# A block kernel of attention and gated feed-forward: its down-projection by seven half-width products, with both LayerNorms of the second branch fed from the chip

## The chip, the cores and the metric

The kernel runs on one core of a Trainium2 chip. The metric is device time in microseconds (us). The five engines have short names in the profile: PE (TensorE; PEld is its weight load), DVE (VectorE), ACT (ScalarE), POOL (GpSimd) and SP (SyncE, which here issues the DMAs).

## The reference

An input of 2048 tokens by 512 columns goes through attention and a gated feed-forward network, each behind a LayerNorm with learned modulation from a condition vector `c`. Keys and values are the last 512 of a cache.

```python
mod = (silu(c) @ w_mod).reshape(1, 6, 1, -1)          # sa, ca, ga, sb, cb, gb
h = layernorm(x) * (1 + ca) + sa
q = h @ wq                                            # 32 heads of 128; 8 key/value heads
p = softmax(q @ k.T * 128 ** -0.5)                    # 512 keys, no mask
x = x + ga * ((p @ v) @ wo)                           # wo: 4096 x 512
h = layernorm(x) * (1 + cb) + sb
x = x + gb * ((gelu(h @ w_gate) * (h @ w_up)) @ w_down)   # feature width 1792
```

## The kernel before

**Numbers.** Every fp32 operand of a matmul is split into a high and a low fp16 half, and each product is three matmuls of 128x128 weights by 512 columns (`mm3`, lines 85 to 88): low by high, high by low, high by high.

**Attention.** The work goes in T = 512 slots of one score tile (128 queries by 512 keys) each, in two halves of 1024 tokens. Slot order is written out by hand for all engines: `at(slot, ...)` puts steps into a slot, `sched(...)` also plans a load into one of five `raw` buffers or two `rw` buffers ahead of it, and three pieces of other PE work are popped in a slot: query projections (seven products in place of eight, on 2x2 blocks), probability by value, and the output projection `y_tasks`. Its sum is added to the accumulator tiles `acc` (128 tokens by 512, eight at a time) on DVE (line 876). When a tile has its last head, `attn_final` stores it as `y1` and later reloads the slot. SP issues all DMAs in program order, so one that waits for its data holds those behind it.

**Work for later stages inside attention.** From slot 286 on, every 27 slots, a pair `n` of feature blocks is prepared: `prep_set` for the gate and the up weights (POOL combinations and splits), `prep_wd` for two row blocks of `w_down`, all stored in DRAM (`kept`). LayerNorm tiles of the first half (`ln_tile` with gen 2) are planned in the same slots: each reloads `y1`, goes through statistics, normalisation on DVE, four PE transposes, modulation on ACT (`affine`), a store to `hs`, and splits. `combos` then makes the sums and differences of the token blocks that the seven products need. Columns of the modulation are made by `mod_load` at slots given in line 1081.

**Feed-forward.** There are 14 pairs: NP = 7 pairs of feature blocks, in each of two passes of 1024 tokens. A pair has two gate/up halves `q` (gate, then up), each of seven products of six matmuls (`f_items`, order 1, 2, 6, 7, 5, 4, 3). GELU runs between ACT and DVE, and the results are split into `at` tiles, keyed 11 and 21 (first token block), 12 and 22 (second). The down-projection of a pair is eight `y_tasks`, one for each 128-token tile, of six 512-column matmuls; `y_next` places one after four of the seven products of a half (line 1523). In the first pass the LayerNorm tiles and combinations of the second 1024 tokens (gen 3) are made too: reload of `y1`, statistics, and so on, with the combinations from gate product 7 on. In this stage the order on all engines but SP is set by the compiler's list scheduling; SP's stays as written. `f_final` stores a finished tile and hands its slot to the next reload. Eight PSUM banks are tagged `acc` (5), `s` (2) and `qa` (1).

Of the kernel before, what the change touches and what calls it, by code (L numbers as in the profile page):

```python
# [63 lines left out]
def block_kernel(ctx: ExitStack, tc: tile.TileContext, x, kT, v, wq, wo, wg, wu, wd, cT, wc, wm, out):  # L64
# [377 lines left out]
    xn = {}  # L442

    def ln_tile(gen, i, src):
# [20 lines left out]
        def affine(dts):  # L465
            if 0 in dts:
                st["f"] = tmp("hf")
# [5 lines left out]
            if KT - 1 in dts:  # L473
                dma(spilled(gen, qb)[:, :, i * P:(i + 1) * P], f.rearrange("p (k q) -> p k q", k=KT))
# [13 lines left out]
        return load, [stat, norm, turn, lambda: affine((0, 1)), lambda: affine((2, 3))] + more  # L488
# [309 lines left out]
    def banks(st, tags):  # L798
        def bk(k):
            def get():  # L800
                if k not in st:
                    st[k] = bank(*tags[k])
                return st[k]
            return get
# [77 lines left out]
    def attn_final(ti):  # L882
# [3 lines left out]
        at(now[0] + 3, lambda: load_acc(nxt, rows_of(x, nxt) if ti < 2 * QT else y1[nxt]))  # L886
# [194 lines left out]
    for j, ts_ in ((3, (257, 261, 265, 269)), (4, (259, 263, 267, 271)), (5, (274, 278, 282, 286))):  # L1081
# [5 lines left out]
    at(("w", 272), lambda: mx.update(m=mod_max(3)))  # L1087
    at(274, lambda: mod_scale(3, "mf", 1.0, mx["m"]))
# [24 lines left out]
    plan_gen(2, [T // 2 + 32 + 27 * (i // 2) + 11 * (i % 2) for i in range(8)], 478, 10, lambda i: y1[i])  # L1113
# [55 lines left out]
    B, A, G = {}, {}, {}  # L1169
# [9 lines left out]
    def f_items(q, hold=None):  # L1179
# [27 lines left out]
        def result(key, src):  # L1207
# [3 lines left out]
            else:  # L1211
                g = G.pop((n, key))
                nc.vector.scalar_tensor_tensor(g, g, 0.5 * GU, src, op0=ALU.mult, op1=ALU.mult)
                t = pair("ot", "at", NOT)
                nc.scalar.activation(t[:, 0, :], g, AF.Copy)
                nc.vector.tensor_tensor(t[:, 1, :], g, t[:, 0, :], op=ALU.subtract)
                A[n, key] = t
# [29 lines left out]
        tags = {"a": ("s", "fa", 2) if q else ("qa", "fa", 1), "b": ("acc", "fb", NACC), "c": ("acc", "fc", NACC)}  # L1247
        return with_posts(("f", q), 2 + q // (2 * NP), banks(st, tags), after)

# [51 lines left out]
    def prep_wd(n, b):  # L1301
        m, st = {}, {}
        outs = [staged() for _ in range(2)]
# [17 lines left out]
        def make(k):  # L1321
            nc.gpsimd.tensor_tensor(st[k], st[k], m["g"], op=ALU.mult)
            halves(outs[k][0]["t"], st[k])

        sched(b, (lambda: load(0), [lambda: stat(0), nop]), b + 7)
        sched(b + 1, (lambda: load(1), [lambda: stat(1), spread, nop]), b + 4, b + 9)
# [9 lines left out]
    for k in range(2):  # L1336
        at(T - 1 + 2 * k, lambda k=k: WO.update({("f", 0, k): fetch(("wd", 0, k), get_wo())}))
# [138 lines left out]
    load_later = []  # L1476
# [13 lines left out]
    for n in range(1, 2 * NP):  # L1490
        for k in range(2):
            f_at(2 * n + 1, 2 * k, lambda n=n, k=k: WO.update({("f", n, k): fetch(("wd", n % NP, k), get_wo())}))
# [74 lines left out]
```

## Time and profile before

| | |
|---|---|
| median of 3 runs | 1769.49 us (1769.39 to 1770.97) |
| profiled execution | 1767.57 us, span 1765.8 us, clock 1.000 |
| last accumulator tile of attention stored (`y1`) | issued at 1370.9 us |
| DVE busy, span | 1442.3 us (82%) |
| ACT busy, span | 1210.3 us (69%) |
| DMA | 329.71 MB, mean 187 GB/s |

The page gives for each engine the busy time within the span, then the span in 40 slices, the DMA queues, the chain of work that ended last, and groups of like instructions with their busy time, the mean of one and the idle time before them. A matmul's duration in the profile is its latency, and matmuls overlap, so their pace is read from start to start. Other views give the same quantities for a stretch of the span, a list in order of time, and who waited for whom.

### The profile page before, as it was taken

To read this page: it belongs to the slowest core of one execution; us is meant where nothing else is said; L and a number is where in the kernel's file an instruction comes from. 1 tells how busy PE (TensorE), PEld (TensorE's weight loads), DVE (VectorE), ACT (ScalarE), POOL (GpSimd) and SP (SyncE) were. 2 spreads that over 40 slices of the span, in tenths; PEclk is the share of its full clock that TensorE was granted. 3 is DMA by queue.
4 is the path that set the end of the run, shared out by engine and by line. 5 is a ranking of instruction groups with operands and counts; after the bars stand their busy time and mean duration, and the time that the engine had idled before them with its cause. 6 is when DMAs were issued, how large, how long until landed. Compare 5 with 4: busy or idle time off the path is not lost.

```text
span 1765.8 us, 25953 instructions
## 1 busy us (share of the span) xinstructions
PE 1730.5 (98%) x8112; PEld 796.0 (45%) x8114; DVE 1442.3 (82%) x2517; ACT 1210.3 (69%) x2814; POOL 875.9 (50%) x1095
## 2 busy tenths in 40 slices
PE   7899999999999999999999999999999999999999
PEld 5444444444444444444444444444444444444443
DVE  7888888888888888988888888888885867766676
ACT  6887787878778777677878777777773455434342
POOL 4879878776788872235475465565520033000000
PEclk9999999999999999999999999999999999999999
DMA  7999998999999989998999999999985543252222
GB/s 230 211 196 212 214 217 200 223 203 219 217 217 229 205 186 196 205 225 200 236 205 219 234 214 200 223 207 208 198 171 141 182 146 111 69 188 75 86 75 75
DMA packets 663273, 329.71 MB, mean 187 GB/s; under 512 B 553184, under 2 KB 575968, under 8 KB 663136
## 3 DMA queue, kind: packets, MB, share of 16 engines
q1 hardware_dynamic: 662848, 327.53, 80.2%
q8 instruction: 64, 1.05, 0.2%
q14 instruction: 73, 0.60, 0.1%
q10 hardware_dynamic: 288, 0.52, 0.1%
HBM read 133.83 MB, written 59.90 MB: 110 GB/s over the span
## 4 chain that ended last, share of the span: by engine, by line
PE 76%; DVE 11%; ACT 5%; POOL 3%; issue 3%; DMA 2%; SPq 0%; POOLq 0%; ACTq 0%; DVEq 0%
PE py L86 7%; PE py L87 7%; PE py L88 7%; PE ps L86 5%; PE ps L88 5%; PE ps L87 5%; PE po L86 4%; PE po L87 4%; PE po L88 4%; DVE p L925 3%; PE fa L86 3%; PE fa L88 2%; PE fa L87 2%; DVE nm L899 2%; PE qa L86 2%
## 5 line engine op out<-in xcount | busy, mean ns | idle before, releaser
L908 ACT ACTIVATE ee<-ps,nm 128x512 f32<-128x512 f32 x512 | 351.2, 686 | 254.1 <-DVE nm L899 244.4
L925 DVE SCALAR_TENSOR_TENSOR p<-ee,rr,p 128x512 f16<-128x512 f32 x512 | 463.4, 905 | 0.2
L899 DVE TENSOR_REDUCE nm<-ps 128x1 f32<-128x512 f32 x512 | 348.8, 681 | 73.5 <-PE ps L88 72.0
L920 ACT ACTIVATE p<-ee,rr 128x512 f16<-128x512 f32 x512 | 365.2, 714 | 1.7 <-DMA pt<-p 1.4
L86 PE MATMUL ps<-k,qt 128*128 128x512 f16 x512 | 194.1, 379 | 16.5 <-DVE qt L668 13.1
L86 PE MATMUL py<-wo,ot 128*128 128x512 f16 x512 | 194.1, 379 | 1.6 <-DVE ot L668 1.6
L86 PE MATMUL po<-pt,v 128*128 128x512 f16 x512 | 194.1, 379 | 0.1
L87 PE MATMUL po<-pt,v 128*128 128x512 f16 x512 | 194.0, 379 | 0.0
L88 PE MATMUL po<-pt,v 128*128 128x512 f16 x512 | 194.0, 379 | 0.0
L87 PE MATMUL py<-wo,ot 128*128 128x512 f16 x512 | 194.0, 379 | 0.0
L88 PE MATMUL py<-wo,ot 128*128 128x512 f16 x512 | 194.0, 379 | 0.0
L88 PE MATMUL ps<-k,qt 128*128 128x512 f16 x512 | 194.0, 379 | 0.0
L87 PE MATMUL ps<-k,qt 128*128 128x512 f16 x512 | 193.9, 379 | 0.0
L916 DVE RECIPROCAL rr<-rr 128x2 f32<-128x2 f32 x256 | 41.5, 162 | 102.7 <-ACT rr L913 101.3
L386 POOL TENSOR_TENSOR rs<-rs,nhalf 128x1 f32<-128x1 f32 x32 | 19.6, 611 | 194.1 <-DVE rs L380 191.5
L86 PEld LDWEIGHTS <-w 128*128 128x128 f16 x728 | 71.2, 98 | 88.4 <-DMA w<-kept 2.9
L87 PEld LDWEIGHTS <-w 128*128 128x128 f16 x728 | 71.2, 98 | 87.3 <-issue 2.7
L88 PEld LDWEIGHTS <-w 128*128 128x128 f16 x728 | 71.2, 98 | 86.0 <-issue 0.2
L876 DVE SCALAR_TENSOR_TENSOR acc<-py,dysc,acc 128x512 f32<-128x512 f32 x112 | 81.6, 746 | 28.8 <-PE py L88 28.0
L876 DVE SCALAR_TENSOR_TENSOR acc<-py,ysc,acc 128x512 f32<-128x512 f32 x128 | 94.6, 739 | 10.9 <-PE py L88 10.9
L908 ACT ACTIVATION_READ_ACCUMULATOR ee<-ps,nm 128x1 f32 x512 | 100.7, 197 | 0.0
L668 DVE SCALAR_TENSOR_TENSOR ot<-po,ot 128x512 f16<-128x512 f32 x128 | 86.9, 679 | 0.0
(263 smaller groups left out, 3817.1 us busy)
## 6 DMA issues: line engine op xcount, KB each, us to landing
w<-kept SPq DMA_DIRECT2D x123, 256.0 KB, 3.2
wo<-kept SPq DMA_DIRECT2D x60, 256.0 KB, 3.6
raw<-in_wo SPq DMA_DIRECT2D x56, 256.0 KB, 3.2
kept<-stage SPq DMA_DIRECT2D x56, 256.0 KB, 3.4
kept<-w SPq DMA_DIRECT2D x39, 256.0 KB, 3.4
rw<-in_wq SPq DMA_DIRECT2D x38, 256.0 KB, 3.3
hs<-hf SPq DMA_DIRECT2D x32, 256.0 KB, 2.7
pt<-p SPq DMA_TRANSPOSE x512, 3.5
```

The source lines that it names most:

```text
L86: nc.tensor.matmul(ps, llo, rhi, start=first, stop=False, skip_group_check=chain)
L87: nc.tensor.matmul(ps, lhi, rlo, start=False, stop=False, skip_group_check=chain)
L88: nc.tensor.matmul(ps, lhi, rhi, start=False, stop=last, skip_group_check=chain)
L386: nc.gpsimd.tensor_tensor(st["rs"], st["rs"], nhalf, op=ALU.pow)
L668: return lambda: nc.vector.scalar_tensor_tensor(t[:, 1, :], src, scale, t[:, 0, :], op0=ALU.mult, op1=ALU.subtract)
L876: nc.vector.scalar_tensor_tensor(acc[ti], st["p"], by, acc[ti], op0=ALU.mult, op1=ALU.add)
L899: nc.vector.tensor_reduce(nm, E[t]["ps"], axis=AX.X, op=ALU.max, negate=True)
L908: nc.scalar.activation(e, E[t]["ps"], AF.Exp, bias=E[t]["nm"], scale=1.0, accum_out=sm[:, t % 2:t % 2 + 1])
L916: return lambda: nc.vector.reciprocal(r, r)
L920: nc.scalar.activation(p16[:, 0, :], E[t]["e"], AF.Copy, scale=E[t]["r"])
L925: nc.vector.scalar_tensor_tensor(p16[:, 1, :], E[t]["e"], E[t]["r"], p16[:, 0, :], op0=ALU.mult, op1=ALU.subtract)
```

## The change

The down-projection of the first six pairs of each pass (`seven(n)`) is done on 2x2 blocks as well: two token blocks, two feature blocks, and two halves of 256 output columns, with seven products instead of eight. `y_sums` forms the four combinations of the results on POOL, `split` makes their fp16 halves on ACT and POOL, and `y_seven` is the list of 14 pieces of six matmuls of 256 columns for a pair, one placed after every product of the next halves from the fifth step on. Three of seven sums are copied from PSUM by ACT and added by POOL in two parts; four are added by DVE, one piece later (`defer`). PSUM banks of the long chains go round `qa`, `s`, `s`. `prep_wd` makes the four combinations of `w_down` and stores four tiles instead of two; the slots of the preparation move.

LayerNorm tiles of gen 2 take the accumulator tile itself, in place, 1 to 13 slots after `attn_final`, with normalisation on ACT; the reload of that slot moves from 3 to 12 slots behind. For gen 3 the statistics are taken at the end of attention (`ln_last`) and kept in `kmax` and `kinv`; normalisation is on ACT. Modulation columns 3 and 4 move from slots 257 to 271 to slots 211 to 229. In the feed-forward stage, the gen 3 stores, the first pass's outputs and its accumulator reloads are put off by 3, 2 and 5 product steps (`put_off`, `tick`), and the gen 3 combinations are spread by 2.5 steps instead of 2.

```diff
...
...
+    def tick():
+        for x in waits_:
+            x[0] -= 1
+        for x in [x for x in waits_ if x[0] <= 0]:
+            waits_.remove(x)
+            x[1]()
+    def ln_last(i):
+        st = {}
+        ln_stat(acc[2 * QT + i], st)
+        ln_power(st)
+        rs, nm = col("kmax", i), col("kinv", i)
+        pool_ts(rs, st["rs"], 1.0)
+        pool_ts(nm, st["mv"][:, 0:1], st["rs"], -1.0)
...
-            st["x"] = raw("xs")
-            dma(st["x"], src())
+            if gen == 2:
+                st["x"] = src()
+            else:
+                st["x"] = raw("xs")
+                dma(st["x"], src())
         def stat():
             ln_stat(st["x"], st)
             ln_power(st)
+            if gen == 2:
+                st["nm"] = small.tile([P, 1], F32, name="nmean")
+                pool_ts(st["nm"], st["mv"][:, 0:1], st["rs"], -1.0)
         def norm():
+            if gen == 3:
+                rs, nm = col("kmax", qb * QT + i), col("kinv", qb * QT + i)
+                return nc.scalar.activation(st["x"], st["x"], AF.Identity, bias=nm, scale=rs)
+            if gen == 2:
+                return nc.scalar.activation(st["x"], st["x"], AF.Identity, bias=st["nm"], scale=st["rs"])
             nc.vector.tensor_scalar(st["x"], st["x"], st["mv"][:, 0:1], st["rs"], op0=ALU.subtract, op1=ALU.mult)
...
-                st["f"] = tmp("hf")
+                st["f"] = raw("hf") if gen == 2 else tmp("hf")
...
+                def spill():
+                    dma(spilled(gen, qb)[:, :, i * P:(i + 1) * P], f.rearrange("p (k q) -> p k q", k=KT))
+                if gen == 3:
+                    put_off(3, spill)
+                else:
+                    spill()
...
+            own, steps = ln_tile(2, ti, lambda: acc[ti])
+            own()
+            for d, fn in zip((1, 6, 8, 9, 10, 12, 13), steps):
+                at(("w", now[0] + d), fn)
+            at(now[0] + 12, lambda: load_acc(nxt, rows_of(x, nxt)))
+        else:
+            ln_last(ti - 2 * QT)
+            at(now[0] + 3, lambda: load_acc(nxt, y1[nxt]))
...
+    for j, ts_ in ((3, (211, 215, 223, 227)), (4, (213, 217, 225, 229)), (5, (274, 278, 282, 286))):
         for dt in range(KT):
...
+    at(("w", 232), lambda: mx.update(m=mod_max(3)))
+    at(234, lambda: mod_scale(3, "mf", 1.0, mx["m"]))
...
-    plan_gen(2, [T // 2 + 32 + 27 * (i // 2) + 11 * (i % 2) for i in range(8)], 478, 10, lambda i: y1[i])
+    for p in range(2):
+        sched_combos(2, p, 482 + 10 * p)
...
+    def seven(n):
+        return n % NP < NP - 1
...
+        g11, g21, g12, g22 = (R.pop((n, k)) for k in ("11", "21", "12", "22"))
+        nc.gpsimd.tensor_tensor(g22, g12, g22, op=ALU.add)
+        nc.gpsimd.tensor_tensor(g12, g11, g12, op=ALU.subtract)
+        nc.gpsimd.tensor_tensor(g11, g22, g11, op=ALU.subtract)
+        nc.gpsimd.tensor_tensor(g21, g21, g11, op=ALU.subtract)
+        box = {}
+        def split(k, src):
+            if "t" not in box:
+                box["t"] = pool.tile([P, 4, 2, QB], F16, tag="pt", name="as", bufs=NPT)
+            t = box["t"][:, k]
+            nc.scalar.activation(t[:, 0, :], src, AF.Copy)
+            nc.gpsimd.tensor_tensor(t[:, 1, :], src, t[:, 0, :], op=ALU.subtract)
+            A[n, f"s{k + 1}"] = t
+        for i, (k, src) in enumerate(((0, g22), (1, g11), (3, g21), (2, g12))):
+            at(("f", 2 * n + 2, 1 + i), lambda k=k, src=src: split(k, src))
...
-                nc.vector.scalar_tensor_tensor(g, g, 0.5 * GU, src, op0=ALU.mult, op1=ALU.mult)
-                t = pair("ot", "at", NOT)
-                nc.scalar.activation(t[:, 0, :], g, AF.Copy)
-                nc.vector.tensor_tensor(t[:, 1, :], g, t[:, 0, :], op=ALU.subtract)
-                A[n, key] = t
+                dst = src if seven(n) and key != "21" else get_qt32() if seven(n) else g
+                nc.vector.scalar_tensor_tensor(dst, g, 0.5 * GU, src, op0=ALU.mult, op1=ALU.mult)
+                R[n, key] = dst
+                if not seven(n) or key != "12":
+                    t = pair("ot", "at", NOT)
+                    nc.scalar.activation(t[:, 0, :], dst, AF.Copy)
+                    nc.vector.tensor_tensor(t[:, 1, :], dst, t[:, 0, :], op=ALU.subtract)
+                    A[n, key] = t
+                if seven(n) and key == "12":
+                    y_sums(n)
...
-        tags = {"a": ("s", "fa", 2) if q else ("qa", "fa", 1), "b": ("acc", "fb", NACC), "c": ("acc", "fc", NACC)}
+        tags = {"a": chain_tag, "b": ("acc", "fb", NACC), "c": ("acc", "fc", NACC)}
...
+    def chain_tag():
+        chains[0] += 1
+        return (("qa", "fa", 1), ("s", "fa", 2), ("s", "fa", 2))[(chains[0] - 1) % 3]
...
+            if not seven(n):
+                halves(outs[k][0]["t"], st[k])
+            elif k == 0:
+                halves(outs[0][0]["t"][:, :, l], st[0][:, l])
+            else:
+                halves(outs[1][0]["t"], st[1])
+                combine()
...
+        def combine():
+            tt(st[0][:, l], st[0][:, r], st[0][:, l])
+            tt(st[0][:, r], st[1][:, r], st[0][:, r])
+            tt(st[1][:, r], st[1][:, r], st[0][:, l])
+            tt(st[1][:, l], st[1][:, l], st[1][:, r])
+        def keep_it(k):
+            t = outs[k][0]["t"]
+            w = slice(0, 256 if seven(n) and k == 0 else 512)
+            store(("wd", n, k), t[:, :, w], 0)
+        last = 11 if seven(n) else 9
+        sched(b + 2, (lambda: load(0), [lambda: stat(0), nop]), b + last)
+        sched(b + 4, (lambda: load(1), [lambda: stat(1), spread, nop]), b + 5, b + last)
         for k in range(2):
-            sched(b + 7 + 2 * k, (outs[k][1], [lambda k=k: make(k), lambda k=k: store(("wd", n, k), outs[k][0]["t"], 0)]), b + 10 + 2 * k)
+            sched(b + 8 + k, (outs[k][1], [lambda k=k: make(k), lambda k=k: keep_it(k)]), b + 12 + k)
+        if seven(n):
+            for k in range(2):
+                sched(b + 10 + k, (outs[2 + k][1], [lambda k=k: halves(outs[2 + k][0]["t"], st[k]), lambda k=k: keep_it(2 + k)]), b + 14 + k)
...
-        prep_set(2 * n + 1, b + 13)
-        prep_wd(n, b + 18)
...
+        prep_set(2 * n + 1, b + 12)
+        prep_wd(n, b + 21)
+    def fetch_wd(n, k):
+        t = get_wo()
+        fetch(("wd", n % NP, k), t[:, :, 0:256] if seven(n) and k == 0 else t)
+        return t
+    for k in range(4):
+        at(T + 7 + k, lambda k=k: WO.update({("f", 0, k): fetch_wd(0, k)}))
...
+    defer = []
     def y_next():
         if nexty:
+            fns = defer[:]
+            defer.clear()
             all_of(nexty.pop(0))
-        if len(load_later) > 2 or load_later and not nexty:
-            t = load_later.pop(0)
-            load_acc(t, y1[t])
+            for fn in fns:
+                fn()
+    YPROD = {1: ("a", "11", 0, 0, "keep", 0, 0), 2: ("b", "21", 1, 0, "add", 0, 0), 5: ("c", "s1", 2, 0, "add", 1, 1),
+             6: ("a", "s2", 3, 1, "keep", 0, 1), 3: ("c", "s4", 1, 1, "add", 0, 1), 7: ("a", "s3", 2, 1, "keep", 1, 1),
+             4: ("a", "22", 3, 0, "add", 1, 0)}
+    def y_seven(n, x):
+        st = {}
+        by = col("dysc", n % NP)
+        def go(k):
+            ch, a, w, h = YPROD[k][:4]
+            if k in (1, 2, 5):
+                st[ch] = bank(*(chain_tag() if ch == "a" else ("acc", "py", NACC)))
+            w, rs = WO["f", n, w], slice(256 * h, 256 * h + 256)
+            for ii in range(2):
+                sl = slice((2 * x + ii) * P, (2 * x + ii + 1) * P)
+                mm3(st[ch][:, 256 * ii:256 * ii + 256], A[n, a][:, 0, sl], A[n, a][:, 1, sl], w[:, 0, rs], w[:, 1, rs],
+                    k in (1, 2, 5) and ii == 0, k in (2, 3, 4) and ii == 1, True)
+        def post(k):
+            ch, what, qi, h = YPROD[k][0], *YPROD[k][4:]
+            src = st[ch]
+            if what == "keep":
+                src = pool.tile([P, 512], F32, tag="rw", name="yk", bufs=NRW)
+                nc.scalar.activation(src, st[ch], AF.Copy, scale=by)
+            for ii in range(2):
+                t = acc[(2 * (n // NP) + qi) * QT + 2 * x + ii][:, 256 * h:256 * h + 256]
+                s_ = src[:, 256 * ii:256 * ii + 256]
+                if what == "keep":
+                    nc.gpsimd.tensor_tensor(t, t, s_, op=ALU.add)
+                else:
+                    defer.append(lambda t=t, s_=s_: nc.vector.scalar_tensor_tensor(t, s_, by, t, op0=ALU.mult, op1=ALU.add))
+        return [[(lambda k=k: go(k), None), (nop, lambda k=k: post(k))] for k in (1, 2, 5, 6, 3, 7, 4)]
     ORDER = (1, 2, 6, 7, 5, 4, 3)
     def f_at(q, k, *fns):
...
-        q = 7 * (7 + 2 * p)
+        q = 49 + 23 * p
...
-                f_at((q + 2 * off) // 7, (q + 2 * off) % 7, fn)
+                f_at((q + 5 * off // 2) // 7, (q + 5 * off // 2) % 7, fn)
     def f_final(ti):
-        dma(rows_of(out, ti), acc[ti])
-        if ti < 2 * QT:
-            load_later.append(ti + 2 * QT)
+        if ti >= 2 * QT:
+            dma(rows_of(out, ti), acc[ti])
+        else:
+            put_off(2, lambda: dma(rows_of(out, ti), acc[ti]))
+            put_off(5, lambda: load_acc(ti + 2 * QT, y1[ti + 2 * QT]))
...
-            if k in (1, 2, 5, 6) or load_later:
-                y_next()
-        if m == 1:
+            tick()
+            y_next()
+        if m == 1 and seven(n):
+            f_at(q + 1, 4, lambda n=n: nexty.extend(y_seven(n, 0) + y_seven(n, 1)))
+        elif m == 1:
...
+    for fn in defer:
+        fn()
+    while waits_:
+        tick()
```

More of the change, by code (lines that the diff above doesn't have):

```diff
@@ L487, in ln_tile @@
         more = [lambda: parts(True), lambda: parts(False)] if gen < 3 else []
-        return load, [stat, norm, turn, lambda: affine((0, 1)), lambda: affine((2, 3))] + more
+        return load, [nop if gen == 3 else stat, norm, turn, lambda: affine((0, 1)), lambda: affine((2, 3))] + more
     def combos(gen, p, eng, base=True, d=0, e=0):
@@ L885, in attn_final @@
         nxt = (ti + 2 * QT) % NT
-        at(now[0] + 3, lambda: load_acc(nxt, rows_of(x, nxt) if ti < 2 * QT else y1[nxt]))
+        if ti < 2 * QT:
+            own, steps = ln_tile(2, ti, lambda: acc[ti])
[6 more added lines that the diff above has]
+            at(now[0] + 3, lambda: load_acc(nxt, y1[nxt]))
     def scores(t):
@@ L1168, in block_kernel, with get_qt32, y_sums @@
     NQ = 4 * NP
-    B, A, G = {}, {}, {}
+    A, G, R = {}, {}, {}
+    def seven(n):
+        return n % NP < NP - 1
+    def get_qt32():
+        return pool.tile([P, QB], F32, tag="qt", name="g21", bufs=3)
+    def y_sums(n):
+        g11, g21, g12, g22 = (R.pop((n, k)) for k in ("11", "21", "12", "22"))
[13 more added lines that the diff above has]
+            at(("f", 2 * n + 2, 1 + i), lambda k=k, src=src: split(k, src))
     def set_srcs(q):
@@ L1302, in prep_wd @@
         m, st = {}, {}
-        outs = [staged() for _ in range(2)]
+        outs = [staged() for _ in range(4 if seven(n) else 2)]
+        l, r = slice(0, 256), slice(256, 512)
         def load(k):
@@ L1490, in block_kernel @@
     for n in range(1, 2 * NP):
-        for k in range(2):
-            f_at(2 * n + 1, 2 * k, lambda n=n, k=k: WO.update({("f", n, k): fetch(("wd", n % NP, k), get_wo())}))
+        for k in range(4 if seven(n) else 2):
+            f_at(2 * n + 1, 1 + k, lambda n=n, k=k: WO.update({("f", n, k): fetch_wd(n, k)}))
     for q in range(3, NQ):
```

18 lines of the change are left out of this document (7 added, 11 removed).

## The prediction

> **What bounds it.** I read the page first, then the groups by shape, then the table of stages, then the chain of waits, and the timeline where one of these raised a question.
>
> ```profile
> span 1765.8 us, 25953 instructions
> ...
> PE 1730.5 (98%) x8112; PEld 796.0 (45%) x8114; DVE 1442.3 (82%) x2517; ACT 1210.3 (69%) x2814; POOL 875.9 (50%) x1095
> ```
> ```profile
> L86 PE MATMUL py<-wo,at 128*128 128x512 f16 x224 | 84.9, 379 | 0.5 <-DVE at L1216 0.5
> ```
> The group is one of three alike (L86, L87, L88): 672 matmuls of 512 columns make up the down-projection, and PE waited 0.5 us in all for their inputs. Its mean of 379 ns is a latency; the pace stands in the timeline of PE and PEld (start, duration, instruction):
>
> ```profile
> 1500.08 0.38 PE L87 MATMUL py<-wo,at 128*128 128x512 f16 x1
> ...
> 1502.88 0.38 PE L88 MATMUL py<-wo,at 128*128 128x512 f16 x1
> ```
> ```profile
> 1500.08 0.10 PEld L88 LDWEIGHTS <-at 128*128 128x128 f16 x1
> ```
> Thirteen matmuls start between these two rows: 2.80 / 13 = 0.2154 us each. The weight load for the next one starts with the matmul before it and takes 0.10, so it is hidden. The table of stages (stretch, its length, then busy time of PE, PEld, DVE, ACT and POOL, clock, DMA share, GB/s) says where PE is not full:
>
> ```profile
> 730.00:740.00 10.00, 8.97 (x42) 3.99 (x41) 9.21 (x18) 7.07 (x17) 4.10 (x4) 1.00 0.77 149
> 820.00:840.00 20.00, 19.10 (x89) 8.15 (x87) 18.05 (x33) 14.56 (x37) 16.10 (x20) 1.00 0.87 204
> 900.00:910.00 10.00, 9.19 (x44) 4.01 (x42) 8.29 (x15) 6.94 (x17) 6.70 (x7) 1.00 1.02 255
> 970.00:980.00 10.00, 9.00 (x44) 4.01 (x42) 8.73 (x16) 5.92 (x16) 5.67 (x6) 1.00 1.00 238
> 690.00:770.00 80.00, 78.97 (x370) 36.12 (x369) 72.44 (x144) 57.80 (x137) 13.37 (x15) 1.00 0.98 217
> 1430.00:1440.00 10.00, 8.47 (x42) 3.97 (x41) 8.04 (x15) 5.21 (x11) 0.55 (x1) 1.00 0.64 215
> 1570.00:1580.00 10.00, 8.19 (x37) 3.42 (x36) 6.88 (x11) 3.98 (x7) 0.00 (x0) 1.00 0.91 305
> 1500.00:1560.00 60.00, 60.00 (x280) 27.20 (x278) 42.40 (x65) 23.77 (x38) 0.00 (x0) 1.00 0.17 55
> ```
> The last row is the feed-forward stage as it mostly looks: PE full, DVE at 71%, ACT at 40%, POOL idle. So in that stage matmul work that goes is time that goes, as long as the three other engines keep up. PE loses 1.53 us at 1430 and 1.81 us at 1570. The chain of waits names the same thing at both places, and SP's own timeline why it came late:
>
> ```profile
> 1427.75 4.28 DMA w<-kept
> ...
> 1574.00 4.51 DMA w<-kept
> ```
> ```profile
> 1408.51 0.45 SPq L94 DMA_DIRECT2D w<-kept  x1
> 1425.39 0.52 SPq L94 DMA_DIRECT2D hs<-hf  x1
> ```
> SP issued nothing for 17 us before the store of a LayerNorm tile, because that tile was not there yet; the weights queued behind it left late.
>
> **Down-projection on PE.** A pair of feature blocks (two gate/up halves of 7 products) now costs 2 x 42 + 48 = 132 matmuls of 512. In 12 of the 14 pairs the 48 become 84 of 256 columns. No fp16 matmul of 256 columns is in the trace. From below it is half of 0.2154, 0.1077. The nearest rows are the fp32 transposes, 128 columns, each with its own weight load:
>
> ```profile
> 1435.97 0.60 PE L463 MATMUL pln<-ident,xs 128*128 128x128 f32 x4
> 1436.41 0.38 PE L86 MATMUL fb<-b,w 128*128 128x512 f16 x1
> ```
> ```profile
> 1435.76 0.58 PEld L463 LDWEIGHTS pln<-ident,xs 128*128 128x128 f32 x4
> ```
> Four pairs of weight load and matmul take 0.44 us, 0.110 each, with loads that are slower than the 0.10 of fp16. From above: if loads queued one behind another as these do (four in 0.58, 0.145 each), 0.145. I take 0.110, the measured pace of PE. Then 48 x 0.2154 = 10.34 becomes 84 x 0.110 = 9.24: 1.10 us a pair, 13.2 us in all (15.5 at 0.1077; break-even is at 0.123). The Trainium skill, "TensorE: Matmul & The Clock Gate", section "Wait — 56ns, not 53.3ns?", speaks against halving: a warm matmul costs a fixed 2.5 ns beside its columns. By that it would be 256 / 2.4 + 2.5 = 109.2 ns, and the gain, an estimate from that page, 14.0 us; 512 / 2.4 + 2.5 = 215.8 agrees with 0.2154.
>
> **What the other engines get for it.** The rows, from the groups by line (busy, mean ns of one):
>
> ```profile
> L876 DVE SCALAR_TENSOR_TENSOR acc<-py,dysc,acc 128x512 f32<-128x512 f32 x112 | 81.6, 746 | 28.8 <-PE py L88 28.0
> L1216 DVE TENSOR_TENSOR at<-fg,at 128x512 f16<-128x512 f32 x56 | 39.7, 709 | 11.8 <-ACT at L1215 10.4
> L809 ACT ACTIVATE fg<-fa 128x512 f32<-128x512 f32 x37 | 22.0, 594 | 56.6 <-PE fa L88 56.4
> L1215 ACT ACTIVATE at<-fg 128x512 f16<-128x512 f32 x56 | 35.1, 628 | 55.6 <-DVE fg L1213 55.5
> L502 POOL TENSOR_TENSOR cb<-cb 128x512 f32<-128x512 f32 x8 | 11.5, 1435 | 0.2
> L367 POOL TENSOR_TENSOR t<-cb,t 128x512 f16<-128x512 f32 x8 | 11.4, 1438 | 0.0
> L367 POOL TENSOR_TENSOR b<-cb,b 128x512 f16<-128x512 f32 x6 | 6.9, 1158 | 28.0 <-ACT b L363 28.0
> ```
> ```profile
> L1269 POOL TENSOR_TENSOR rw<-rw 128x256 f32<-128x256 f32 x56 | 48.6, 868 | 4.1
> ```
> A pair is to last 84 x 0.2154 + 9.24 = 27.3 us. DVE: 8 adds of 0.746 become 16 of 256 columns. Their price lies between 0.373 and 0.746; POOL's ratio of 256 to 512 columns, 868 / 1435, gives 0.45. That is 7.2 for 6.0, less one split of 0.709: +0.5, hidden in its 29% of idle time. ACT: six copies out of PSUM at 0.594 and three splits more at 0.628: +5.4 us, in 60% idle. POOL, idle until now: 4 sums x 1.435, 4 splits x 1.438, 12 adds x 0.868: 21.9 us of 27.3.
>
> POOL is where it can fail. In the first pass it also prepares the next operand, whose rows are the last three of 512 columns: 11.5 + 11.4 + 6.9 = 29.8 us. The change spreads them from gate product 7 on, and product 14 needs them: 7 x 13.65 = 95.6 us, in which POOL would have 3.5 x 21.9 + 29.8 = 106.5. Some 11 us too much. Part is taken up by slack ahead of the splits; between 0 and 11 I take 6 us of stall. Second pass: none.
>
> New waits on queues. ACT's copies queue ahead of gate copies and wait for one of two buffers that POOL's adds free; a late POOL so holds ACT, then PE's banks. DVE's adds to a tile wait for POOL's adds to the same half; queued behind them on DVE are gate results. Both belong to the POOL case below. Stores, outputs and accumulator reloads in this stage are put off by two to five product steps; that is what takes SP's waits at 1430 and 1570 away: -3.3 us. Four weight fetches a pair instead of two, in a stage whose DMA share was 0.17: nothing; without that cover, two transfers of 4.3 us.
>
> **Attention.** Second LayerNorm straight from the accumulator:
>
> ```profile
> L471 ACT ACTIVATE hf<-pln,cols 128x128 f32<-128x128 f32 x96 | 37.9, 462 | 1.6 <-PE pln L463 1.6
> ...
> L483 ACT ACTIVATE b<-hf 128x256 f16<-128x256 f32 x24 | 9.2, 425 | 0.0
> ...
> L405 ACT ACTIVATE xn<-acc,nmean 128x512 f32<-128x512 f32 x2 | 1.4, 722 | 0.9 <-DVE nmean L383 0.9
> ```
> ```profile
> 687.85 0.73 DVE L876 SCALAR_TENSOR_TENSOR acc<-py,ysc,acc 128x512 f32<-128x512 f32 x1
> ...
> 757.95 0.74 DVE L876 SCALAR_TENSOR_TENSOR acc<-py,ysc,acc 128x512 f32<-128x512 f32 x1
> ```
> The eight tiles of the first half end between these two rows, one every 10 us, and now each brings its LayerNorm at once: 0.722 + 4 x 0.462, and two parts of 0.425 for four tiles, one for the others, 25.7 us on ACT. With the 57.8 of the stretch from 690 to 770 that is 83.5 in 80: 3.5 us too much at worst, nothing if the last tile's steps run past 770, as their offsets say. DVE gets the statistics there and loses the modulation columns:
>
> ```profile
> L135 DVE SCALAR_TENSOR_TENSOR wmc<-wmc,sbc 128x512 f32<-128x512 f32 x12 | 8.6, 716 | 0.0
> ```
> Eight of these, 5.7 us, move to before 600 us; PE idle there covers none of it, DVE's own slack does, and it is 5.7 us at most. The dips at 730, 820, 900 and 970 (1.03 + 0.90 + 0.81 + 1.00 = 3.7 us) stand where weights are prepared beside LayerNorm tiles; the new slots may end them, and the four combinations a pair on POOL may bring them back. Traffic: +384 KB of stores a pair, eight reloads of 256 KB less, a net 0.3 MB, 1.2 us at 217 GB/s, under a DMA share of 0.98. I take 0 for attention, from -3.7 to +5.
>
> **Sum.** -13.2 - 3.3 + 6 + 0 = -10.5 us. The profiled execution took 1767.57 us, 1.8 beyond its span, so 1757.1; the median of the runs is 1.9 higher: 1759.0.
>
> **Rivals.** *All of it arrives*: POOL's late operands are covered and the dips go: -13.2 - 3.3 - 3.7 = -20.2, 1749.3. For it: PE stayed at 10.00 in most of the old stage with DVE, ACT in long chains. Against: the 106.5 in 95.6.
>
> *POOL and DVE block each other, slower.* Timeline of DVE, then of POOL:
>
> ```profile
> 1483.88 1.64 DVE L1202 SCALAR_TENSOR_TENSOR fg<-sq,fg 128x512 f32<-128x512 f32 x1
> 1485.44 1.75 DVE L1216 TENSOR_TENSOR at<-fg,at 128x512 f16<-128x512 f32 x1
> ...
> 1489.57 0.68 DVE L1195 SCALAR_TENSOR_TENSOR sq<-sq,fg 128x512 f32<-128x512 f32 x1
> ```
> ```profile
> 1479.35 1.27 POOL L502 TENSOR_TENSOR cb<-cb 128x512 f32<-128x512 f32 x1
> ...
> 1484.93 1.71 POOL L502 TENSOR_TENSOR cb<-cb 128x512 f32<-128x512 f32 x1
> ```
> While POOL runs, a DVE operation with both inputs in SBUF takes 1.64 to 1.75 instead of 0.68, and POOL's 1.27 becomes 1.71: they take turns. A pair has 12 such DVE operations. POOL's sums begin when the last product has passed DVE, three operations of 0.7 or 2.1 us into the next half; before the sixth item of the down-projection, nine steps of 1.95 and one product of 1.29 later (18.9), it must finish four sums, four splits and six adds of 0.868. That holds up to a mean of (18.9 - 2.1 - 5.2) / 8 = 1.45 us a large operation. The mean of the rows is 1.435, in turns it is 1.71: then 2.1 us late a pair, 12 x 2.1 = 25, and -16.5 + 25 = +8.7: 1778. The Trainium skill, "SBUF — State Buffer", section "SBUF: two separate sides", calls the pair of ports that DVE and POOL share an exclusive lock, held for the whole instruction; these rows agree (1.64 = 0.68 and most of a POOL operation). Against it: PE stood at full through these very microseconds, but with POOL's results needed much later.
>
> *The two cancel*: about 15 us of stalls, within 3.5 us of before.
>
> *Weight loads set the pace*, 0.145: 84 x 0.145 = 12.2 for 10.34, +22 us, less 3.3: 1788 or more.
>
> **Chances.** Forecast 0.48, all of it 0.24, cancelling 0.09, POOL 0.14, weight loads 0.03, attention worse by more than the gain 0.02. About 0.2%, 3.5 us, is what a measurement can tell: faster 0.72, same 0.09, slower 0.19. The range goes from 1747 (0.1077 a matmul and every dip gone) to 1776, short of the POOL rival; about 0.07 lies below and 0.13 above.
>
> **What would show it.** Right: 1008 matmuls of 128x256 starting 0.110 apart, a last attention tile as early as before, no `w<-kept` in the chain at the two places, POOL near 80% over the second stage, and PE's idle time there mostly between gate products 8 and 14 behind POOL. Wrong: a pace above 0.123; waits of `py` on POOL in every pair; L1202, L1213 and L1216 at means over 1.2 us with DVE full; or new dips at 690 to 770 and before 600.

## The result, and the profile after

The changed kernel takes 1815.52 us (median of 4 runs, 1811.74 to 1819.96) where the kernel before took 1769.44: ratio 1.0259, 95% interval 1.0245 to 1.0273. The forecast was 1759.0, the range 1747 to 1776. The profiled execution took 1816.9 us, span 1815.1, which is 49.3 us more than before.

The head of the page after:

```profile
span 1815.1 us, 27486 instructions
...
PE 1735.4 (96%) x8546; PEld 839.4 (46%) x8546; DVE 1489.7 (82%) x2585; ACT 1280.7 (71%) x2938; POOL 1166.4 (64%) x1407
...
PE 47%; DVE 17%; POOL 15%; ACT 11%; issue 6%; DMA 4%; SPq 0%; POOLq 0%; ACTq 0%; DVEq 0%
```

The last line is the chain that ended last by engine. POOL holds 15% of it although it is busy for only 64% of the span. To see where the time went, the two stages are taken apart at the last of the 512 score tiles, by the start of its row reduction on DVE (timeline, before and then after):

```profile
1330.01 0.69 DVE L899 TENSOR_REDUCE nm<-ps 128x1 f32<-128x512 f32 x1 [0.52 <-PE ps L88]
```
```profile
1371.15 0.69 DVE L945 TENSOR_REDUCE nm<-ps 128x1 f32<-128x512 f32 x1 [0.52 <-PE ps L88]
```

So attention lost 41.1 us, and what follows took 444.0 us instead of 435.8, 8.2 more. The same reduction of every tile gives a lag for each slot (after minus before): 0.8 us at slot 192, 7.2 at 240, 12.6 at 304. From slot 327 on come six stalls of some 4 to 6 us, about 27 slots apart, up to 41.9 at slot 464.

**One stall.** The table of stages of the kernel after (stretch, length, busy PE, PEld, DVE, ACT, POOL, clock, DMA share, GB/s):

```profile
860.00:870.00 10.00, 10.00 (x48) 4.51 (x47) 9.36 (x14) 6.69 (x16) 9.43 (x11) 1.00 0.76 184
870.00:880.00 10.00, 5.83 (x27) 2.45 (x25) 3.14 (x7) 3.92 (x10) 6.31 (x8) 1.00 0.40 107
880.00:890.00 10.00, 9.56 (x38) 4.06 (x39) 8.30 (x16) 7.85 (x20) 1.53 (x4) 0.83 1.14 234
```

PE, DVE and ACT all stop together, and the granted clock falls behind it. Now the timelines of POOL, SP and ACT at this place:

```profile
853.58 3.91 POOL L1417 TENSOR_TENSOR raw<-raw 128x256 f32<-128x256 f32 x4
...
860.23 1.16 POOL L157 TENSOR_TENSOR stage<-raw,stage 128x512 f16<-128x512 f32 x1
...
862.49 1.16 POOL L157 TENSOR_TENSOR stage<-raw,stage 128x512 f16<-128x512 f32 x1
...
869.57 3.47 POOL L1353 TENSOR_TENSOR rw<-rw 128x256 f32<-128x256 f32 x4
...
873.83 1.15 POOL L157 TENSOR_TENSOR stage<-rw,stage 128x512 f16<-128x512 f32 x1
```
```profile
867.30 1.24 SPq L975 DMA_TRANSPOSE pt<-p  x1
875.01 0.34 SPq L94 DMA_DIRECT2D rw<-in_wu  x1
```
```profile
871.49 0.69 ACT L705 ACTIVATE qt<-qd,qsc 128x512 f16<-128x512 f32 x1
878.05 0.63 ACT L216 ACTIVATE junk<-rw 128x512 f16<-128x512 f32 x1 [5.88 <-DMA rw<-in_wu]
878.59 0.19 ACT L216 ACTIVATION_READ_ACCUMULATOR junk<-rw 128x1 bf16 x1
878.68 0.19 ACT L959 ACTIVATE rr<-sm 128x2 f32<-128x2 f32 x1
```

POOL works almost without a gap from 846.5 to 876.8 us. The four `w_down` combinations (L1417) and their splits stand ahead of the next pair's gate weights. The split of these ends at 874.98, and only then is the `rw` buffer free. SP issues the load of the up weights at 875.01, having held its queue, transposes of probabilities included, since 868.5. The weights arrive at 878.03. Meanwhile ACT stands at the statistic of that tile (L216), its next instruction in order, with the softmax behind it (L959). Who waited for whom, in the stretch from 866 to 882:

```profile
DVE rr L962 <- ACT rr L959: 7.2, 2, 6.9
ACT junk L216 <- DMA rw<-in_wu: 5.9, 1, 5.9
PEld L86 <- DVE qt L706: 5.1, 1, 5.1
```

A load that is late by POOL stops ACT, ACT stops DVE, DVE stops PE.

**Before the stalls.** Stages from 600 us, before and then after, and a line of the second LayerNorm's stretch after:

```profile
600.00:640.00 40.00, 39.90 (x186) 18.01 (x185) 34.09 (x58) 29.17 (x70) 33.42 (x40) 1.00 0.93 206
```
```profile
600.00:650.00 50.00, 47.05 (x219) 20.94 (x217) 46.81 (x85) 34.69 (x82) 39.05 (x45) 1.00 0.93 207
690.00:780.00 90.00, 88.19 (x421) 41.40 (x420) 77.35 (x146) 75.41 (x184) 34.47 (x46) 1.00 0.91 200
```

With the modulation columns in slots 211 to 229, DVE goes from 85% to 94%, and PE loses 2.95 us in 50. In the chain of waits from 585 to 615 the columns (`wmc`, L135) hold 13.2%: they are on the path. In the LayerNorm's stretch ACT goes from 72% to 84%.

**The feed-forward stage.** The table of stages from the end of the scores to the end, cut between the passes, before and then after:

```profile
1330.00:1571.00 241.00, 237.62 (x1115) 109.47 (x1114) 169.42 (x268) 108.62 (x190) 34.36 (x30) 1.00 0.42 131
1571.00:1765.80 194.80, 188.71 (x872) 84.78 (x869) 132.43 (x201) 73.19 (x115) 0.00 (x0) 1.00 0.29 95
```
```profile
1371.20:1612.00 240.80, 224.58 (x1279) 125.06 (x1278) 180.84 (x290) 139.25 (x246) 162.69 (x166) 0.99 0.42 130
1612.00:1815.10 203.10, 194.11 (x1139) 110.81 (x1137) 154.06 (x256) 107.48 (x175) 121.39 (x120) 1.00 0.36 115
1490.00:1520.00 30.00, 25.60 (x155) 14.69 (x153) 25.47 (x37) 16.68 (x29) 30.00 (x28) 1.00 0.28 93
1520.00:1550.00 30.00, 25.01 (x152) 14.70 (x152) 23.55 (x32) 18.10 (x31) 29.58 (x25) 1.00 0.41 128
```

The cuts are at equal times and not at equal work, but PE's idle time is plain: 3.4 us became 16.2 in the first part, 6.1 became 9.0 in the second. The worst is from 1490 to 1550, where the gen 3 combinations lie: POOL full, PE idle for 9.4 us of 60. Here are PE's longest waits of the first pass, and the groups on DVE and POOL in the stage:

```profile
PE fa L86 <- ACT fg L847: 3.8, 5, 1.0
PE py L86 <- POOL as L1238: 2.0, 3, 1.3
PE fa L86 <- ACT yk L1626: 1.9, 2, 1.0
PE fa L86 <- DVE g L1287: 1.7, 2, 1.4
PE fa L86 <- DVE acc L1633: 1.7, 3, 1.1
PE fc L86 <- DVE acc L1633: 1.6, 1, 1.6
```
```profile
L1633 DVE SCALAR_TENSOR_TENSOR acc<-py,dysc,acc 128x256 f32<-128x256 f32 x144 | 66.1, 477 | 35.7 <-POOL acc L1631 31.1
L1268 DVE SCALAR_TENSOR_TENSOR sq<-sq,fg 128x512 f32<-128x512 f32 x42 | 42.9, 1022 | 21.5 <-ACT sq L1265 21.3
L1275 DVE SCALAR_TENSOR_TENSOR fg<-sq,fg 128x512 f32<-128x512 f32 x42 | 40.0, 953 | 6.9 <-ACT sq L1271 6.7
```
```profile
L1631 POOL TENSOR_TENSOR acc<-acc,yk 128x256 f32<-128x256 f32 x144 | 122.6, 876 | 72.9 <-ACT yk L1626 69.3 <-DVE acc L1633 2.0 <-DVE u L1258 1.6
...
L1238 POOL TENSOR_TENSOR as<-u,as 128x512 f16<-128x512 f32 x24 | 29.5, 1232 | 0.0
L1229 POOL TENSOR_TENSOR fu<-u,fu 128x512 f32<-128x512 f32 x12 | 17.1, 1428 | 0.1
```

No single wait carries it. Each engine waits a little for the next one, and DVE sat 31.1 us behind POOL's adds to the same halves.

### The profile page after: what moved, and what is told of

Its sections match the earlier page's. It is cut to its first block, busy times and chain, and to the rows that moved or that the text cites. A ratio compares the mean times of both kernels' runs of the same rounds, so it can differ in the third digit from the quotient of the medians.

```text
span 1815.1 us, 27486 instructions
## 1 busy us (share of the span) xinstructions
PE 1735.4 (96%) x8546; PEld 839.4 (46%) x8546; DVE 1489.7 (82%) x2585; ACT 1280.7 (71%) x2938; POOL 1166.4 (64%) x1407
## 4 chain that ended last, share of the span: by engine, by line
PE 47%; DVE 17%; POOL 15%; ACT 11%; issue 6%; DMA 4%; SPq 0%; POOLq 0%; ACTq 0%; DVEq 0%
DVE p L971 5%; PE py L86 4%; PE py L87 4%; PE py L88 4%; DVE nm L945 3%; PE ps L86 3%; PE ps L88 3%; PE ps L87 3%; PE po L88 3%; PE po L86 3%; PE po L87 3%; ACT ee L954 3%; POOL acc L1631 2%; ACT p L966 2%; POOL stage L157 2%
## 5 line engine op out<-in xcount | busy, mean ns | idle before, releaser
L971 DVE SCALAR_TENSOR_TENSOR p<-ee,rr,p 128x512 f16<-128x512 f32 x512 | 478.0, 934 | 0.2
L86 PE MATMUL ps<-k,qt 128*128 128x512 f16 x512 | 195.1, 381 | 38.5 <-DVE qt L706 25.2
L1631 POOL TENSOR_TENSOR acc<-acc,yk 128x256 f32<-128x256 f32 x144 | 122.6, 876 | 72.9 <-ACT yk L1626 69.3
L87 PEld LDWEIGHTS <-w 128*128 128x128 f16 x728 | 71.8, 99 | 89.8 <-issue 14.4
L233 POOL TENSOR_TENSOR lw<-lw,half__86 128x1 f32<-128x1 f32 x37 | 21.0, 568 | 136.3 <-DVE lw L183 136.2
L1633 DVE SCALAR_TENSOR_TENSOR acc<-py,dysc,acc 128x256 f32<-128x256 f32 x144 | 66.1, 477 | 35.7 <-POOL acc L1631 31.1
```

The costliest lines, as they stand in the source:

```text
L86: nc.tensor.matmul(ps, llo, rhi, start=first, stop=False, skip_group_check=chain)
L87: nc.tensor.matmul(ps, lhi, rlo, start=False, stop=False, skip_group_check=chain)
L971: nc.vector.scalar_tensor_tensor(p16[:, 1, :], E[t]["e"], E[t]["r"], p16[:, 0, :], op0=ALU.mult, op1=ALU.subtract)
L1631: nc.gpsimd.tensor_tensor(t, t, s_, op=ALU.add)
L1633: defer.append(lambda t=t, s_=s_: nc.vector.scalar_tensor_tensor(t, s_, by, t, op0=ALU.mult, op1=ALU.add))
```

## The experiments

All run against the kernel before. "Lag" is that of the last score tile, "stage" the time from there to the end, both from the one profiled execution of each kernel. The lag already reads -0.1 to 2.5 us at slot 64, where all of them still do the same work (from 80 to 92 us the clock reads 0.86 in the kernel after and in e6, 1.00 in the kernel before and in e2). So two lags of the table that are 2 us apart show no difference by themselves; what a lag grows by from slot to slot does.

| run | median us | ratio (95%) | lag | stage |
|---|---|---|---|---|
| after | 1815.52 | 1.0259 (1.0245 to 1.0273) | 41.1 | 444.0 |
| e1_no_wd_combos | 1783.27 | 1.0068 (1.0048 to 1.0088) | 9.6 | 443.4 |
| e2_wd_earlier | 1783.88 | 1.0076 (1.0060 to 1.0092) | 6.9 | 444.5 |
| e3_mod_spread | 1820.63 | 1.0280 (1.0258 to 1.0301) | 44.5 | 444.5 |
| e4_lows_on_dve | 1817.76 | 1.0267 (1.0244 to 1.0290) | 41.2 | 448.5 |
| e5_keep_on_dve | 1777.04 | 1.0044 (1.0029 to 1.0059) | 8.1 | 438.5 |
| e6_eight | 1779.89 | 1.0056 (1.0039 to 1.0073) | 9.5 | 438.6 |
| e7_old_ln | 1781.74 | 1.0069 (1.0054 to 1.0084) | 6.9 | 442.6 |
| e8_old_ln_eight | 1775.21 | 1.0035 (1.0022 to 1.0047) | 5.9 | 437.0 |
| e9_second_pass | 1777.40 | 1.0045 (1.0032 to 1.0058) | 8.2 | 436.8 |
| e10_second_old_ln | 1777.31 | 1.0041 (1.0029 to 1.0054) | 6.7 | 436.0 |
| e11_prep_before | 1779.67 | 1.0066 (1.0054 to 1.0078) | 10.0 | 437.6 |
| e12_prep_before_add7 | 1778.10 | 1.0052 (1.0040 to 1.0065) | 9.5 | 436.8 |

**e1_no_wd_combos**: the combinations of `w_down` are left out, with their two splits and stores.

```diff
                 halves(outs[1][0]["t"], st[1])
-                combine()
```

> Leaves out, in attention, the four combinations of w_down, the two extra splits and the two extra stores of each pair (about 10 us of POOL a pair); two of the four stored tiles are the second one again. Theory A (POOL gets to the next gate weights late, SP waits for their buffer, and the probability transposes behind that wait stand still): the six stalls of 4 to 5.5 us at every 27th slot of the second half go, 1815.5 becomes about 1787. Theory B (POOL and DVE block each other at their shared port wherever POOL works more): POOL's time in the second half falls by a sixth, the loss is spread, gain about 8 us, 1807. Theory C (the feed-forward stage alone decides): no change, 1815.

The lag fell from 41.1 to 9.6. The combinations bring the six stalls.

**e2_wd_earlier**: the same work, four slots earlier.

```diff
-        prep_wd(n, b + 21)
+        prep_wd(n, b + 17)
```

> All the work of the changed kernel, with the preparation of w_down four slots earlier (b + 17 for b + 21), so that its POOL work falls between the up set of its pair and the gate set of the next. Theory A: the gate set is no longer late, the six stalls go, about 1787. Theory B: the same POOL and DVE work, so the same blocking, about 1815. If it is the extra transfers, also 1815.

Nothing is left out here, and 31.6 us are gone. The same place in its table of stages:

```profile
860.00:870.00 10.00, 10.00 (x48) 4.56 (x47) 8.99 (x16) 7.14 (x18) 9.27 (x11) 1.00 0.73 173
870.00:880.00 10.00, 10.00 (x49) 4.58 (x48) 7.20 (x14) 7.60 (x21) 0.81 (x1) 1.00 1.10 239
```

SP's waits for POOL's splits between 860 and 1300 us (in all, times, longest), after and then e2:

```profile
SPq L94 <- POOL stage L157: 42.7, 14, 7.2
```
```profile
SPq L94 <- POOL stage L157: 16.5, 16, 2.4
```

ACT's waits for the load of the up weights in the same stretch, after and then e2:

```profile
ACT junk L216 <- DMA rw<-in_wu: 34.9, 10, 5.9
```
```profile
ACT junk L216 <- DMA rw<-in_wu: 7.6, 9, 2.3
```

In the kernel after there is one of 4.7 to 5.9 us in each of the six stalls.

So it is the place of POOL's work, not its amount, that cost most of the lag: from slot 304 on it grows by 28.5 us in the kernel after and shrinks by 4.3 in e2, 33 us apart. e1 alone could not say that.

**e3_mod_spread**: modulation columns 3 and 4 spread over slots 89 to 201.

```diff
-    for j, ts_ in ((3, (211, 215, 223, 227)), (4, (213, 217, 225, 229)), ...
+    for j, ts_ in ((3, (89, 121, 153, 185)), (4, (105, 137, 169, 201)), ...
```

> The eight loads and column sums of modulation 3 and 4 go to slots 89, 105, ... 201, one every 16, in place of 211 to 229. The scores of the changed kernel fall behind those of before by 7 us between slots 208 and 240. If the eight DVE sums on a full DVE are the cause, 6 to 7 us go, about 1809; if it is something else of those slots (the extra buffers, or the scale of slot 232), under 2 us, 1814.

No gain, and neither expectation: the lag ends 3.4 us higher. It now rises step by step with the columns, from 1.3 us at slot 88 to 6.7 at slot 204, 0.7 for each of eight. So there a column costs about its own duration (0.716), and no DVE slack takes it in. From slot 208 to 240 the lag still grows by 3.7 us with no column left there, against 6.1 in the kernel after. What brings these 3.7 is not shown; `mod_max` and `mod_scale` stand in these slots in both.

**e4_lows_on_dve**: the low halves of the gen 3 combinations on DVE instead of POOL.

```diff
-        for load, steps in combos(3, p, nc.gpsimd):
+        for load, steps in combos(3, p, nc.vector):
```

> The fourteen low halves of the gen 3 combinations (first pass of the feed-forward stage) go from POOL to DVE: about 18 us less on POOL, 10 more on DVE. Theory P (POOL is full in the first pass, 106.5 us of work in 95.6): PE's stalls between 1480 and 1560 shrink by 8 to 12 us, about 1805. Theory D (DVE is what holds up the first pass, waiting for POOL's port): no gain or some loss, 1815 to 1820.

The stage grew by 4.5 us. POOL fell to 82% between 1490 and 1550, DVE rose to 89%, and PE still idled 8.2 us of these 60. Moving this work from POOL to DVE is no cure.

**e5_keep_on_dve**: on e2, the three kept sums are added by DVE straight from PSUM, with no copy on ACT and no add on POOL.

```diff
-            if what == "keep":
-                src = pool.tile([P, 512], F32, tag="rw", name="yk", bufs=NRW)
-                nc.scalar.activation(src, st[ch], AF.Copy, scale=by)
...
-                    nc.gpsimd.tensor_tensor(t, t, s_, op=ALU.add)
+                    nc.vector.scalar_tensor_tensor(t, s_, by, t, op0=ALU.mult, op1=ALU.add)
```

> e2 with the three kept sums of each half-pair added straight from PSUM by DVE (two adds of 256 columns each) instead of an ACT copy and two POOL adds: POOL loses 12 adds of 0.87 us a pair (10.5 us), ACT six copies, DVE gains 12 adds of 0.48 (5.7 us). Theory P (one in-order POOL queue of adds, sums and splits sets the feed-forward stage, 444.5 us in e2 from the last score on): the stage comes down by 10 to 16 us, to about 430, the whole to 1770. Theory D (DVE, slowed by taking turns with POOL, sets it): DVE has more to do, the stage stays at 440 to 450, the whole at 1783 or more.

The stage gained 6.0 us on e2. Then DVE is the full one, where the gen 3 combinations lie:

```profile
1458.00:1488.00 30.00, 28.39 (x162) 15.42 (x160) 29.41 (x50) 14.51 (x25) 21.86 (x16) 1.00 0.26 80
```

**e6_eight**: on e2, eight products of 512 columns in all pairs. The rest of the change stays, without combinations.

```diff
     def seven(n):
-        return n % NP < NP - 1
+        return False
```

> e2 with the ordinary down-projection of six 512-column matmuls a tile in all 14 pairs; the LayerNorms, the put-off transfers and all slots stay as changed. If the seven products in their present form cost more than they save: the feed-forward stage takes 432 to 436 us from the last score on (435.8 before, less the 3.3 us of SP waits), attention stays 5 to 7 us behind, the whole is about 1772 to 1775. If the seven products do save the 13 us of matmul time and something else of the stage was lost, it is slower than e2: 1795.

Stage 438.6: the seven products as written cost 5.9 us (444.5 with them), though they take some 14 us of matmuls away. And with eight products, the put-off transfers and the statistics taken earlier should have given 3.3 against before; they lose 2.8. Two DVE groups of the stage in e6:

```profile
L1275 DVE SCALAR_TENSOR_TENSOR fg<-sq,fg 128x512 f32<-128x512 f32 x42 | 30.2, 719 | 11.0 <-ACT sq L1271 9.5
L1268 DVE SCALAR_TENSOR_TENSOR sq<-sq,fg 128x512 f32<-128x512 f32 x42 | 30.1, 716 | 10.3 <-ACT sq L1265 9.9
```

L1268 takes 716 ns here, where POOL is busy for 38.0 us of the stage, and 1022 in the kernel after, where it is busy for 284.1. L1275 takes 719 and 953. There are 42 of each.

**e7_old_ln**: on e5, both LayerNorms, the reloads and the modulation slots of the kernel before.

```diff
-            own, steps = ln_tile(2, ti, lambda: acc[ti])
...
+        at(now[0] + 3, lambda: load_acc(nxt, rows_of(x, nxt) if ti < 2 * QT else y1[nxt]))
```

> e5 with both LayerNorms, their reloads and the modulation columns as before the change (statistics and normalisation of reloaded tiles on DVE, the columns in slots 257 to 271). If the early modulation columns and the LayerNorm burst behind the accumulators cost the 6 to 8 us by which e2 is behind at slot 300: attention ends within 2 us of before, and the whole is 5 us below e5. If the reloads collide with the four w_down tiles in the five buffers: new stalls every 27 slots, 5 to 20 us above e5.

At slot 304 the lag is 1.7 instead of e5's 11.6, so the new LayerNorm with its columns costs 10 us up to there. But it gives 5 back by slot 400 (6.7), where the old one loses 4 (6.0). At the end of the scores the two are 1.2 us apart. The stage is 4.1 slower than e5's. So the first expectation failed: e7 is 4.7 us slower than e5, not 5 faster.

**e8_old_ln_eight**: on e7, eight products, with the adds and banks of e6.

> The changed kernel without its three main parts: eight products (no combinations of w_down), LayerNorms and modulation slots as before; what is left of the change are the moved slots of the preparation (prep_wd at b + 17), the put-off transfers and the PSUM tags. Theory C, the four combinations a pair are what puts 4 us on slots 336 to 384 where the LayerNorms are the old ones: the last score tile within 3 us of before, feed-forward stage 436 to 439 us, in all 1769 to 1773 us. Rival, the moved slots do it: the last score tile 6 to 7 us late, in all 1774 to 1777 us.

The stage is 437.0, as expected. The lag of 5.9 is nearer to the rival, but 1.9 of it is there at slot 64 already. Even without any combinations it goes from 1.9 at slot 304 to 5.0 at slot 400, so these are not all of it.

**e9_second_pass** and **e10_second_old_ln**: on e2, seven products in the second pass only (the first `w_down` tile is then split and stored at full width, for the eight products of the first pass); e10 also with the old LayerNorms and modulation slots.

```diff
-        return n % NP < NP - 1
+        return NP <= n < 2 * NP - 1
```

> e2 (preparation of w_down four slots earlier) with the seven products in the second pass only; the first pass has eight, from the same stored tiles. Theory A, the seven products lose where POOL also makes the second LayerNorm's operand, and pay where it does not: from the end of the scores to the end 433 to 436 us (438.6 with eight in both passes, less 6 x 1.10, plus 1 to 3 us of new stalls), in all 1775 to 1778 us. Rival B, they lose as much in either pass: about 441.5 us (halfway between 438.6 and 444.5), in all 1781 to 1783 us.

> As e9 (seven products in the second pass only), with both LayerNorms, the reloads and the modulation slots as before. Theory A: attention about 7 us late at its last score tile, as in e7, the stage after it 433 to 436 us, in all 1772 to 1775 us, so still behind the kernel before. Rival B: stage of 440 to 443 us, in all 1780 to 1783 us.

Stages of 436.8 and 436.0, just above and within 433 to 436. With eight in the first pass the stage is 7.7 us shorter than e2's, so it is there that the seven products lose. In the second pass they gain 1.8 (e9 against e6) or 1.0 (e10 against e8) of 6.6, each from one execution. PE's idle time in the stage shows most of the rest: 14.7 us in e9 for 10.8 in e6. e10's total came out 2 us above its range, and 2.1 above e8's: from slot 304 on its lag grows by 6.1 us, where e8's grows by 4.0. In the medians the seven products gain nothing here.

**e11_prep_before** and **e12_prep_before_add7**: on e10, the preparation in the slots of the kernel before with the combinations behind it; e12 also adds product 7 on DVE.

```diff
-        prep_set(2 * n + 1, b + 12)
-        prep_wd(n, b + 17)
+        prep_set(2 * n + 1, b + 13)
+        prep_wd(n, b + 18)
```

> As e10 (seven products in the second pass, LayerNorms and modulation slots as before), with the preparation back in the slots of the kernel before (second set at b + 13, w_down at b + 18, its products at +7 and +9) and the four combinations right behind, at +10 and +11, three slots ahead of the next pair's first set. Theory, the 4 to 5 us of slots 336 to 384 in e8 and e10 belong to the moved slots: last score tile 1 to 3 us late, stage after it 435 to 437 us, in all 1770 to 1773 us. Rival, they stay: 6 to 7 us late, 1775 to 1778 us.

> e11 with the sums of product 7 added by DVE straight from PSUM (no copy on ACT, no add on POOL). POOL falls from about 70% to 57% of the second pass, DVE rises from 78% to 85%. Theory, the 5 us of stalls that e9 and e10 have in the middle of the second pass come from POOL's queue: stage after the scores 432 to 434 us, in all 1767 to 1771 us, level with the kernel before. Rival, DVE becomes the limit as in e5: 436 to 438 us, 1771 to 1775 us.

Both theories fell. In the old slots the lag grows from 3.0 at slot 304 to 10.1 at 384, more than in e10 (0.6 to 4.6): the change's other spacing of the preparation makes room for the combinations. One product's adds moved to DVE gave 0.8 us of stage, and the intervals of the two runs overlap. None of the versions is faster than the kernel before.

## Why the prediction was wrong

**The price of a 256-column product was right.** The timeline of PE after, first and last of 18 starts in a row:

```profile
1433.74 0.27 PE L86 MATMUL py<-wo,at 128*128 128x256 f16 x1
...
1435.59 0.27 PE L88 MATMUL fa<-wo,as 128*128 128x256 f16 x1
```

1.85 / 17 = 0.1088 us, for a forecast of 0.110 and 0.1092 by the Trainium skill, "TensorE: Matmul & The Clock Gate", section "Wait — 56ns, not 53.3ns?", which this trace bears out. With 576 matmuls of 0.2154 gone and 1008 of 0.1088 in their place, 14.4 us was there to be had, a little more than the forecast's 13.2, and weight loads set no pace.

**The step that failed is "I take 0 for attention, from -3.7 to +5".** Attention lost 41.1 us. The chances had this outcome, "attention worse by more than the gain", at 0.02, with no mechanism and no price.

- *Dips beside the preparation*: the sentence that the four combinations "may bring them back" named the right cause, and priced it at the old dips, 3.7 us in all. With the preparation where the change puts it, they cost 33 us (e2). What was missing is the step from POOL's order to the `rw` load and ACT's statistic on it, 4.7 to 5.9 us of waiting for the late load in each of the six stalls.
- *Modulation columns*: "DVE's own slack" hides none of them where they stand alone: eight cost 5.4 us by the lag in e3, close to the 5.7 that were given as a ceiling. Slots 208 to 240 cost 6.1 in the kernel after, and 3.7 in e3 without the columns. The sum had nothing for these 3.7.
- *LayerNorm from the residual*: 12.6 - 8.5 = 4.1 us of lag in slots 272 to 304, as the 3.5 of the ACT count said "at worst"; part comes back later (e7 against e5).

**The feed-forward stage was forecast 10.5 us shorter and is 8.2 longer.** With 14.4 us of matmul work gone, PE then lost 22.6 us more between matmuls than before. 15.7 of them show as idle time of PE in the table above. The rest does not: a 256-column matmul is shown with a latency of 0.27 at a pace of 0.109, so a gap behind it shows only beyond 0.16 us, and the clock reads 0.99 over the first part.

- *POOL's stall in the first pass, +6*: the stretch named, gate products 7 to 14, is where POOL is full and PE idles 9.4 us. But the whole first part has 16.2 us of idle PE for 3.4, and e2 against e9 prices the seven products there at +7.7 net: 7.2 of gain at the measured pace and some 15 of loss. The sum counted POOL's work by itself and left out that DVE's operations grow beside it: L1268 from 716 to 1022 ns, L1275 from 719 to 953.
- *Second pass, no stall*: 1.0 to 1.8 us arrived of 6.6.
- *The two SP waits, -3.3*: not seen as a gain. In the first pass PE waits for no `w<-kept` any more, but 1.4 us of it stand at 1637.7, early in the second pass. The same put-off transfers with eight products give stages of 438.6 and 437.0 us (e6, e8) for 435.8.

**The rival that POOL and DVE block each other** put the loss in every pair at 25 us, if POOL's large operations came to 1.71 us. The sums and splits came to 1.23 to 1.43 by group, under the 1.45 where that would begin, and the small loss of the second pass fits this. It was right in kind for the first pass only, and its signs did not come as named. L1202, L1213 and L1216, which are L1275, L1287 and L1292 now, take at most 0.95, 0.81 and 0.94 us by group, below the 1.2 named, and PE's `py` waited for POOL three times in the first part and twice in the second, not in every pair. Of the signs for the forecast, the pace held. The last attention tile, POOL's 80% (64% of the stage) and the place of PE's idle time (9.4 of 25.2 us in the worst stretch) did not. Of the new dips named as a sign of being wrong, those before 600 us came (PE idles 1.9 us from 560 to 600, 0.5 before), those at 690 to 770 did not (0.8 us for 1.0).

What stays open: which edge gives the 3 us of slots 304 to 400 in e8, where neither the combinations nor the new LayerNorm are present; and, in the first pass, how much of the 15 us is POOL's queue and how much the longer DVE operations. e4 and e5 moved work from the one to the other, and each time PE lost in the same stretch. The longer DVE operations alone do not make the loss: in e9 the two of e6 above take 738 and 744 ns in the first pass and 931 and 979 in the second, where the seven products still gain a little.

## What to carry to other kernels

Work added to an engine at half load is free only where it stands behind everything that others wait for. Ask which buffer its queue gives back late, what load that holds, and which in-order engine has an instruction planned on that load. Saved matmuls are worth what the slowest of the helping engines leaves of them: add up DVE and POOL together, with the longer durations that each has beside the other, for the pass that has most other work.

## What the runs showed of the hardware

After PE's stop of 4.6 us at 876, the granted clock read 0.83 from 880 to 890 us; in the kernel before no stop after the first 20 us is longer than 2.7 us, and the clock is 1.00 in all its stages shown. The Trainium skill, "TensorE: Matmul & The Clock Gate", section "What's actually happening", has an idle window of about 3.4 us halve the clock until the array has been busy as long. 3.4 us at half speed in 10 would read 0.83, so the trace agrees with the length. That a stop must fill such a window it does not bear out: one of 2.4 us, up to 1026.9, was followed by a clock of 0.66 from 1027 to 1032, while one of 3.1 us, up to 1248.3, left it at 1.00 from 1245 to 1253. Adding 256 columns from PSUM on DVE takes 0.477 us for 0.746 of 512 columns, so halving the columns saves about a third and not a half.
